# A long kernel transposed by the DMA crossbar, and 62 instead of 54 pairs of score tiles exponentiated on VectorE

## The chip, the cores and the metric

The kernel runs on one core of one Trainium2 chip. The core has five engines with their own instruction streams: TensorE (PE: matmuls and weight loads), VectorE (DVE), ScalarE (ACT), GpSimd (POOL) and SyncE (SP, which here only issues DMAs). The metric is the device time of one execution in microseconds. Before the change it is 924.57 us, the median of three runs (921.49 to 927.49).

## The reference, cut to what matters

The input `x` (2048 tokens, 640 features, bf16) goes through two branches, which a gate mixes token by token. Branch A multiplies a short causal convolution of `k` with `v`, and then convolves the product along the tokens with a kernel as long as the sequence, one for each feature (`ssm_k`, 640 x 2048). Branch B is attention with 32 heads of 20 features that share one key and one value.

```python
g = sigmoid((x * gate_w).sum(-1, keepdims=True))
# A: kv = shortconv(k) * v;  y = causal_conv(kv, ssm_k) (by FFT in the reference) + kv * ssm_D;  a = x * y
# B:
q = (x @ wq).reshape(B, S, 32, 20).transpose(0, 2, 1, 3)
k = x @ wk                                   # one key, one value for all heads
v = x @ wv
p = softmax(einsum("bhqd,bkd->bhqk", q, k) * 20 ** -0.5)
b = einsum("bhqk,bkd->bhqd", p, v).transpose(0, 2, 1, 3).reshape(B, S, 640) @ wo
return g * a + (1 - g) * b
```

## The kernel before

A Python program builds a graph of all operations with priorities and estimated costs, simulates the engines, and so fixes the order of the instructions on each engine before anything runs. On the chip each engine goes through its list in that order; an instruction whose input is late holds up all behind it.

The scores are made transposed, 128 keys by 512 queries of one head: a tile. A group is one block of 512 queries and four heads. There are 4 blocks and 8 sets of heads, so 32 groups, each with 16 key blocks `j` for each of its 4 heads: 2048 tiles in all. ScalarE takes most of them through `exp`, in units of three and two tiles by turns:

```python
n = 2 if len(self.units) % 2 else 3
...
op("act", lambda e: e.activation(et(n)[:, 0:w], self.ps[:, lo:lo + w], ACT.Exp, scale=SCALE), ...)   # L1056
```

TensorE writes the scores (`score`, L1024) into PSUM banks 0 to 2 and 3 to 4 and multiplies the exponentials with the values (`PVmm`, L1098) into bank 6, which collects one group. The banks 5 and 7 are for everything else.

Some key blocks of a group have two of their four heads on VectorE. `DVE_J[G]` lists these blocks. A pair is computed with integer and floating-point steps that build `exp` from an exponent and a polynomial, 128 x 1024 elements at a time:

```python
DVE_J = [()] * 5 + [(2, 9)] * 27
...
def DEXP(G, j):
    ...
        self.evac(gr, "dve", ...tensor_scalar(J[:, 512*h:512*h+512], self.bank(bk), ...))      # L1086, twice
    V(tensor_scalar(E, J, 7, 0x7F800000, logical_shift_left, bitwise_and), ...)                # L1089
    V(scalar_tensor_tensor(Ef, lo, ED, Ef, ALU.add, ALU.mult), ...)                            # L1091
    V(scalar_tensor_tensor(Jf, lo, EP, lo, ALU.add, ALU.mult), ...)                            # L1093
    V(scalar_tensor_tensor(T["ETd"], Jf, EQ, Ef, ALU.add, ALU.mult), ...)                      # L1094
```

There are two buffers `dJ`, one `dE` and one `ETd`. The value products of a pair may come at any point after the group's first one and must come before its last one (`late_pv`). When a group is full, VectorE copies bank 6 to `acc` (L1152), the denominators go through three small DMAs (`den`, `scr_d`, `rbc`), and VectorE scales the result (L1164).

The long convolution is done by discrete Fourier transforms, that is matmuls with tables of cosines and sines, in five blocks `c` of 128 features. It needs `ssm_k` with the tokens on the partitions. Each block is loaded as it lies, transposed on TensorE and copied out of PSUM by VectorE:

```python
def ssm_kT(self, c, base):
    p = c % 2
    st, kt = T["kst0"], T[f"ssm_kT{p}"]
    self.dma(st[:, :], self.aps["A_ssm_k"][CW*c:CW*c+CW, :], writes=[("kst", 0)], nbytes=524288, prio=base - 100, ...)
    for blk in range(2):
        gr = self.group("sk", base - 20 + blk)
        for n in range(NF):                                    # 8 transposes of 128 x 128, L1290
            self.mm(gr, lambda e, bk, ...: e.transpose(self.bank_bf(bk, 128, 128*n), st[:, j0:j0+128], T["ident"]), ...)
        self.evac(gr, "dve", ... e.tensor_copy(out, self.bank_bf(bk, 1024)), (), [("ssm_kT", p)], 0.7)   # L1293
```

The spectra (L1344, evicted by L1355, L1361 and L1363 on VectorE), their products (L1375, on GpSimd) and the inverse (L1408) follow, as side work between the exponentials. Two other inputs come in through transposing DMAs (`dma_start_transpose`) already: `xT` (L723) and `kTr` (L1254). Where TensorE has no side work, fillers (L1490: matmuls with zeros) stand in.

Of the kernel before, what the change touches and what calls it, by code (L numbers as in the profile page):

```python
# [10 lines left out]
BF16 = dt.bfloat16  # L11
# [486 lines left out]
S, D, H, DH = 2048, 640, 32, 20  # L498
NSC, NDC, NB = 16, 5, 4
L = 2048  # L500
NF = 8
CW = 128
# [7 lines left out]
UP = 256.0  # L510

SIDE = (7, 5)
DVE_J = [()] * 5 + [(2, 9)] * 27
MAC_ALT = ()
SCALE = float(DH) ** -0.5

# [25 lines left out]
class Kernel:  # L542

    def __init__(self, nc, aps):
        self.nc = nc
        self.aps = aps
        self.g = Graph()
        self.T = {}
        self.late_pv = []
# [52 lines left out]
    def alloc(self):  # L602
        nc = self.nc
        T = self.T

        def sb(name, shape, dtype):
            T[name] = nc.alloc_sbuf_tensor(name, shape, dtype)

        def size(shape, dtype):
            n = mybir.dt.size(dtype)  # L610
            for s in shape[1:]:
                n *= s
            return (n + 31) // 32 * 32

        def region(name, *sets):
# [3 lines left out]
            for st in sets:  # L619
                off = base  # L620
                for n, s, d in st:
                    T[n] = nc.alloc_sbuf_tensor_at(n, s, d, offset=off)
                    off += size(s, d)
# [55 lines left out]
        spec = []  # L679
# [2 lines left out]
        spec += [("Pp", [128, 3, 2, 2, CW], F32)]  # L682
        for i in range(2):
            spec += [(f"ssm_kT{i}", [128, 2, NF, CW], BF16)]
        spec += [("kst0", [128, S], BF16)]
        last = [("wo", [128, NDC, D], BF16), ("oTp0", [128, NDC, 512], BF16), ("oTp1", [128, NDC, 512], BF16)]
        last += [(f"outsb{i}", [128, D], BF16) for i in range(4)]
        region("R2", keep + early0, keep + early, spec + late, last)
        def over(name, under, off, shape, dtype):
            T[name] = nc.alloc_sbuf_tensor_at(name, shape, dtype, offset=nc.lookup_mloc(T[under]).addr + off)  # L690

# [2 lines left out]
        over("wog", "wq_pad", 0, [128, 8, D], BF16)  # L694
        self.fam0 = [n for n, _, _ in early0]
        self.early_fams = [n for n, _, _ in early + keep]
        self.late_fams = ["AB", "X", "K", "Pp", "ssm_kT", "kst"]
        self.spec_fams = ["X", "K", "Pp", "ssm_kT", "kst"]
        self.last_fams = ["wo", "oTp", "outsb"]
        self.ps = nc.alloc_psum_tensor("ps", [128, 4096], F32)  # L700
        self.ps_bf = self.ps[:, :].bitcast(BF16)
# [4 lines left out]
    def loads(self):  # L706
        T, aps = self.T, self.aps
        x = aps["A_q"][0].rearrange("(i p) d -> p i d", p=128)
        self.dma(T["wkv"][:, :, 0:20], aps["B_wk"].rearrange("(dc p) c -> p dc c", p=128), writes=["wk"],
                 nbytes=50000, eng="act", prio=-98.8)  # L710
        self.dma(T["wkv"][:, :, 20:40], aps["B_wv"].rearrange("(dc p) c -> p dc c", p=128), writes=["wv"],
                 nbytes=50000, eng="act", prio=-98.7)
        wq = aps["B_wq"].rearrange("(dc p) n -> p dc n", p=128)
        self.dma(T["gw5"][:, :], aps["gate_w"].rearrange("(dc p) -> dc p", p=128), writes=["gw5"], nbytes=2000,
                 eng="act", prio=-98.65)
        self.dma(T["wqst"][:, :, 0:160], wq[:, :, 0:160], writes=[("wqst", 0)], nbytes=204800, eng="act", prio=-98.6)
        xl = None
        x = aps["A_q"][0].rearrange("(i p) d -> p i d", p=128)
        self.dma(T["xn"][:, 12:16, :], x[:, 12:16, :], writes=[("xn", 3)], nbytes=655360, prio=-9)
        for b in range(NB - 1):  # L720
            o = T["xT"][:, :, 512 * b:512 * b + 512]
            i = aps["A_q"][0][512 * b:512 * b + 512, :]
            xl = self.g.add("sp", lambda e, o=o, i=i: e.dma_start_transpose(o, i), (), [("xT", b)], 0.1, kind="d",  # L723
                            nbytes=655360, prio=-8 + b, lat=1.6)
            xl.iss = 3.3

        self.xl = [xl]
        self.dma(T["wqst"][:, :, 160:640], wq[:, :, 160:640], writes=[("wqst", 1)], nbytes=614400, prio=-4,
                 after=self.xl)
        self.dma(T["Dbc"][:, :], aps["A_ssm_D"].partition_broadcast(128), writes=["Dbc"], nbytes=163840, prio=30,  # L730
                 after=self.xl)
# [262 lines left out]
    def stream(self):  # L994
# [4 lines left out]
        for G in range(8 * NB):  # L999
            for j in range(NSC):  # L1000
                mine = order
                if j in DVE_J[G]:
                    mine, rest = order[:2], order[2:]
# [11 lines left out]
    def attention(self):  # L1015
# [87 lines left out]
        def PV(G, j, rs):  # L1103
# [13 lines left out]
            if j == 0:  # L1117
                for jd in DVE_J[G]:
                    DEXP(G, jd)
# [158 lines left out]

    def ssm_kT(self, c, base):

        T = self.T
        p = c % 2
        st, kt = T["kst0"], T[f"ssm_kT{p}"]
        self.dma(st[:, :], self.aps["A_ssm_k"][CW * c:CW * c + CW, :], writes=[("kst", 0)], nbytes=524288,
                 prio=base - 100, name="ld_ssmk")
        for blk in range(2):
            gr = self.group("sk", base - 20 + blk)
            for n in range(NF):
                j0 = 128 * (NF * blk + n)
                self.mm(gr, lambda e, bk, n=n, j0=j0: e.transpose(self.bank_bf(bk, 128, 128 * n), st[:, j0:j0 + 128],  # L1290
                                                                  T["ident"][:, :]), [("kst", 0), "ident"], 0.09)
            out = kt[:, 1 - blk, :, :].rearrange("p n c -> p (n c)")
            self.evac(gr, "dve", lambda e, bk, out=out: e.tensor_copy(out, self.bank_bf(bk, 1024)), (),  # L1293
                      [("ssm_kT", p)], 0.7)

    def conv(self):
        T = self.T
# [251 lines left out]
```

## Time and profile before

| | before |
|---|---|
| measured, median of 3 (lowest to highest) | 924.57 us (921.49 to 927.49) |
| profiled span | 916.6 us |
| busy: TensorE, VectorE, ScalarE, GpSimd | 862.6, 572.5, 894.3, 369.0 us |
| wide and narrow exponentials on ScalarE | 388 and 388 |
| pairs on VectorE | 54 |
| transposes of the long kernel on TensorE | 80, 7.9 us busy |
| their copies on VectorE | 10, 6.9 us busy |

How to read the profile: a row of groups names the line of the program, the engine, the operation, the written and read tiles with their shapes, the count, the busy time and the mean duration; behind the second bar stands the time that the engine sat idle just before these instructions and what ended it. A row of waits reads "who waited <- for whom: total us, times, longest". A row of the timeline has start, duration, engine, line and operation, and in square brackets the idle time just before. A row of the windows has the stretch, then the busy time and number of instructions of PE, PEld (weight loads), DVE, ACT and POOL, then the granted clock, the DMA share and GB/s. The profiled span leaves out part of what the measured time holds, so the two are not compared with one another.

### The profile page before, as it was taken

Reading aid. Unit: us, or ns where it says so; the run is one execution under the profiler, and the core shown is the slowest. Engines: PE = TensorE matmul, PEld = TensorE weight load, DVE = VectorE, ACT = ScalarE, POOL = GpSimd, SP = SyncE. Lnnn points to the kernel's source line nnn. Section 1 sums busy time; section 2 is a strip of 40 time slices with the busy share of each in tenths; the row PEclk is TensorE's granted clock in tenths of the full one; section 3 lists DMA queues with packets and bytes.
Section 4 is the critical chain, followed back from the end, with each engine's and each line's share of the span. In section 5 each row is a group of like instructions: output and inputs, shape, how many; then the busy total and the mean of one; then the engine's idle time right before and its main releaser. Section 6 shows DMA issues by size and latency. Waiting matters only on the chain.

```text
span 916.6 us, 16425 instructions
## 1 busy us (share of the span) xinstructions
PE 862.6 (94%) x7024; PEld 355.5 (39%) x7086; DVE 572.5 (62%) x816; ACT 894.3 (98%) x800; POOL 369.0 (40%) x330
## 2 busy tenths in 40 slices
PE   7999999999999999999999999999999999988997
PEld 3344444443433434443343343433444333422332
DVE  6457743577666766567866777566676664466642
ACT  5999999999999999999999999999999999999995
POOL 2930055683234386234386234677243673000000
PEclk9999999999999999999999999999999999999999
DMA  7930100010000010000010010000000003002111
GB/s 161 205 128 6 56 28 20 14 31 18 18 19 20 14 35 15 19 20 19 15 38 10 28 46 19 14 18 9 18 20 19 13 14 85 23 28 63 34 34 37
DMA packets 48667, 32.69 MB, mean 36 GB/s; under 512 B 30674, under 2 KB 43986, under 8 KB 48594
## 3 DMA queue, kind: packets, MB, share of 16 engines
q1 hardware_dynamic: 46328, 31.05, 12.0%
q8 instruction: 55, 0.90, 0.4%
q10 hardware_dynamic: 2266, 0.59, 0.3%
q14 instruction: 18, 0.15, 0.1%
HBM read 20.64 MB, written 6.02 MB: 29 GB/s over the span
## 4 chain that ended last, share of the span: by engine, by line
ACT 59%; PE 34%; SPq 2%; DVE 2%; DMA 2%; issue 0%; DVEq 0%
ACT ETA L1056 36%; ACT ETB L1056 23%; PE ps L1024 10%; PE ps L1344 8%; PE ps L1098 7%; PE ps L1408 4%; PE ps L950 2%; SPq L1254 1%; PE ps L1271 1%; DVE ETd L1094 1%; DMA kTr<-in_A_k_dram 1%; PE ps L1188 1%; PE ps L1442 1%; DMA xT<-in_A_q_dram 1%; PE ps L966 1%; SPq L723 1%
## 5 line engine op out<-in xcount | busy, mean ns | idle before, releaser
L1056 ACT ACTIVATE ETA<-ps 128x1536 bf16<-128x1536 f32 x388 | 579.7, 1494 | 3.4 <-PE ps L1024 1.8
L1056 ACT ACTIVATE ETB<-ps 128x1024 bf16<-128x1024 f32 x388 | 417.7, 1077 | 0.0
L1024 PE MATMUL ps<-qT,kT 21*128 21x512 bf16 x2048 | 308.7, 384 | 33.2 <-ACT ETA L1056 16.3
L1375 POOL TENSOR_TENSOR Pp<-X,K 128x512 f32<-128x512 bf16 x120 | 163.3, 1386 | 355.9 <-DVE K L1363 354.7
L1098 PE MATMUL ps<-ETB,vaug 128*32 128x512 bf16 x776 | 200.2, 389 | 0.0
L1098 PE MATMUL ps<-ETA,vaug 128*32 128x512 bf16 x1164 | 191.7, 390 | 0.3 <-ACT ETB L1056 0.2
L1024 PEld LDWEIGHTS ps<-qT,kT 21*128 21x128 bf16 x2048 | 76.0, 91 | 215.4 <-ACT ETA L1056 114.8
L1094 DVE SCALAR_TENSOR_TENSOR ETd<-dJ,dE 128x1024 bf16<-128x1024 f32 x54 | 77.7, 1439 | 27.7 <-PE ps L1098 27.5
L1086 DVE TENSOR_SCALAR dJ<-ps 128x512 uint32<-128x512 f32 x108 | 74.1, 686 | 32.7 <-PE ps L1024 32.1
L1375 POOL TENSOR_TENSOR AB<-Pp 128x256 bf16<-128x256 f32 x80 | 78.0, 975 | 5.8
L1408 PE MATMUL ps<-AB,Tcos 128*128 128x256 bf16 x320 | 78.6, 275 | 0.2 <-issue 0.2
L1098 PEld LDWEIGHTS ps<-ETA,vaug 128*32 128x32 bf16 x1164 | 47.6, 92 | 66.6 <-issue 64.8
L1091 DVE SCALAR_TENSOR_TENSOR dE<-dJ,dE 128x1024 f32<-128x1024 uint16 x54 | 72.9, 1350 | 0.1
L1408 PE MATMUL ps<-AB,Tsin 128*128 128x256 bf16 x280 | 70.0, 275 | 0.0
L1093 DVE SCALAR_TENSOR_TENSOR dJ<-dJ 128x1024 f32<-128x1024 uint16 x54 | 68.4, 1267 | 0.1
L1098 PEld LDWEIGHTS ps<-ETB,vaug 128*32 128x32 bf16 x776 | 48.3, 93 | 47.1 <-issue 46.9
L1375 POOL TENSOR_TENSOR Pp<-Pp 128x512 f32<-128x512 f32 x40 | 57.4, 1434 | 3.1
L1152 DVE COPY acc<-ps 128x512 f32<-128x512 f32 x31 | 21.4, 691 | 58.9 <-PE ps L1098 58.9
L1344 PE MATMUL ps<-ssm_kT,Tcos 128*128 128x256 bf16 x320 | 53.0, 275 | 0.1
L1344 PE MATMUL ps<-kv,Tsin 128*128 128x256 bf16 x320 | 52.7, 275 | 0.0
L1344 PE MATMUL ps<-ssm_kT,Tsin 128*128 128x256 bf16 x320 | 52.7, 275 | 0.0
L1344 PE MATMUL ps<-kv,Tcos 128*128 128x256 bf16 x320 | 52.1, 275 | 0.4 <-DVE dJ L1086 0.4
(138 smaller groups left out, 842.4 us busy)
## 6 DMA issues: line engine op xcount, KB each, us to landing
rbc<-scr_d SPq DMA_DIRECT2D x31, 256.0 KB
scr_o<-oTn SPq DMA_DIRECT2D x24, 128.0 KB, 1.7
xn<-in_A_q_dram SPq DMA_DIRECT2D x4, 640.0 KB
kv<-in_A_v_dram SPq DMA_DIRECT2D x4, 640.0 KB
kst<-in_A_ssm_k_dram SPq DMA_DIRECT2D x5, 512.0 KB
out_dram<-outsb SPq DMA_DIRECT2D x14, 160.0 KB, 1.8
oTp<-scr_o SPq DMA_DIRECT2D x12, 160.0 KB, 3.3
wog<-in_B_wo_dram SPq DMA_DIRECT2D x4, 200.0 KB
```

The costliest lines, as they stand in the source:

```text
L950: o = self.mm(gr, lambda e, bk, gi=gi, dc=dc: e.matmul(self.bank(bk), T["wq_pad"][:, dc, 128 * gi:128 * gi + 128], T["xT"][:, dc, 512 * I: ...
L1024: return e.matmul(self.bank(bk), T["kT4"][32 * r:32 * r + 21, 128 * j:128 * j + 128], T[f"qT{G // 8 % 2}"][32 * r:32 * r + 21, G % 8, :], ...
L1056: op("act", lambda e: e.activation(et(n)[:, 0:w], self.ps[:, lo:lo + w], ACT.Exp, scale=SCALE), [("ps", base[n % 2] + k) for k in range(le ...
L1086: self.evac(gr, "dve", lambda e, bk, h=h: e.tensor_scalar(J[:, 512 * h:512 * h + 512], self.bank(bk), SCALE * LOG2E * 65536.0, EOFF * 6553 ...
L1091: V(lambda e: e.scalar_tensor_tensor(Ef, lo, ED, Ef, ALU.add, ALU.mult), [kJ, "dE"], ["dE"], c_ps(1024), **k)
L1093: V(lambda e: e.scalar_tensor_tensor(Jf, lo, EP, lo, ALU.add, ALU.mult), [kJ], [kJ], c_ps(1024), **k)
L1094: V(lambda e: e.scalar_tensor_tensor(T["ETd"][:, :], Jf, EQ, Ef, ALU.add, ALU.mult), [kJ, "dE"], ["ETd"], c_ps(1024), **k)
L1098: return op("pe", lambda e: e.matmul(self.bank(6)[32 * r:32 * r + 32, :], T["vaug"][:, j, :], src, start=(j == 0), stop=(j == NSC - 1), ti ...
L1152: self.dve(lambda e: e.tensor_copy(T["acc"][:, :], self.bank(6)), [("ps", 6)], ["acc"], c_ps(512), prio=-9000.0, name="acc")
L1344: o = self.mm(gr, lambda e, bk, lhs=lhs, rhs=rhs, comp=comp, n=n: e.matmul(self.bank(bk, 256, 256 * comp), lhs, rhs, start=(n == 0), stop= ...
L1375: f = lambda e: e.tensor_tensor(out, a, b, alu)
L1408: self.mm(gr, lambda e, bk, lhs=lhs, fc=fc, comp=comp, h=h: e.matmul(self.bank(bk, 256, 256 * h), lhs, AB[:, fc, :, comp, :], start=(fc == ...
```

## The change

Two things change. First, the long kernel is loaded by transposing DMAs straight from DRAM into `ssm_kT`, two of 128 features by 1024 tokens for each block; the staging tile `kst0`, the transposes on TensorE and the copies on VectorE go. Second, `DVE_J` gives VectorE 62 pairs instead of 54, and no longer the same two key blocks in each group: groups 3 and 5 get one pair, group 6 four, groups 7, 12, 23, 27, 28, 30 and 31 three, group 22 one, and the other groups from 8 on two. It is meant to relieve ScalarE, and to make room for that on VectorE and TensorE.

```diff
-DVE_J = [()] * 5 + [(2, 9)] * 27
+DVE_J = [(), (), (), (6,), (), (2,), (3, 7, 11, 13), (2, 6, 11), (2, 9), (2, 9), (2, 9), (2, 9), (3, 8, 13), (2, 9), (2, 9), (2, 9), (2, 9), (2, 9), (4, 11), (2, 9), (3, 9), (2, 9), (2,), (3, 8, 13), (2, 9), (2, 7), (2, 9), (2, 7, 12), (3, 8, 13), (3, 9), (3, 8, 13), (2, 7, 12)]
@@ alloc
-        spec += [("kst0", [128, S], BF16)]
@@ ssm_kT
-        st, kt = T["kst0"], T[f"ssm_kT{p}"]
-        self.dma(st[:, :], self.aps["A_ssm_k"][CW * c:CW * c + CW, :], writes=[("kst", 0)], nbytes=524288, ...)
         for blk in range(2):
-            gr = self.group("sk", base - 20 + blk)
-            for n in range(NF):
-                j0 = 128 * (NF * blk + n)
-                self.mm(gr, lambda e, bk, n=n, j0=j0: e.transpose(...), [("kst", 0), "ident"], 0.09)
-            out = kt[:, 1 - blk, :, :].rearrange("p n c -> p (n c)")
-            self.evac(gr, "dve", lambda e, bk, out=out: e.tensor_copy(out, self.bank_bf(bk, 1024)), ...)
+            o = self.T[f"ssm_kT{p}"][:, 1 - blk, :, :]
+            i = self.aps["A_ssm_k"][CW * c:CW * c + CW, 1024 * blk:1024 * blk + 1024]
+            x = self.g.add("sp", lambda e, o=o, i=i: e.dma_start_transpose(o, i), (), [("ssm_kT", p)], 0.1, kind="d",
+                           nbytes=262144, prio=base - 100, lat=1.9, name="ld_ssmk")
+            x.iss = 1.5
```

(The lists of tile families lose `kst` too.)

More of the change, by code (lines that the diff above doesn't have):

```diff
@@ L696, in alloc @@
         self.early_fams = [n for n, _, _ in early + keep]
-        self.late_fams = ["AB", "X", "K", "Pp", "ssm_kT", "kst"]
-        self.spec_fams = ["X", "K", "Pp", "ssm_kT", "kst"]
+        self.late_fams = ["AB", "X", "K", "Pp", "ssm_kT"]
+        self.spec_fams = ["X", "K", "Pp", "ssm_kT"]
         self.last_fams = ["wo", "oTp", "outsb"]
@@ L1279, in ssm_kT @@
     def ssm_kT(self, c, base):
-        T = self.T
         p = c % 2
-        st, kt = T["kst0"], T[f"ssm_kT{p}"]
-        self.dma(st[:, :], self.aps["A_ssm_k"][CW * c:CW * c + CW, :], writes=[("kst", 0)], nbytes=524288,
-                 prio=base - 100, name="ld_ssmk")
         for blk in range(2):
-            gr = self.group("sk", base - 20 + blk)
-            for n in range(NF):
-                j0 = 128 * (NF * blk + n)
-                self.mm(gr, lambda e, bk, n=n, j0=j0: e.transpose(self.bank_bf(bk, 128, 128 * n), st[:, j0:j0 + 128],
-                                                                  T["ident"][:, :]), [("kst", 0), "ident"], 0.09)
-            out = kt[:, 1 - blk, :, :].rearrange("p n c -> p (n c)")
-            self.evac(gr, "dve", lambda e, bk, out=out: e.tensor_copy(out, self.bank_bf(bk, 1024)), (),
-                      [("ssm_kT", p)], 0.7)
+            o = self.T[f"ssm_kT{p}"][:, 1 - blk, :, :]
[3 more added lines that the diff above has]
+            x.iss = 1.5
     def conv(self):
```

## The prediction

> **What bounds the kernel now.** I read the page first (shares, slices, the largest groups), then ScalarE's waits, then the starts of all 776 exponentials in order of time, then VectorE's rows and one stretch where ScalarE did stall. The page:
>
> ```profile
> span 916.6 us, 16425 instructions
> PE 862.6 (94%) x7024; PEld 355.5 (39%) x7086; DVE 572.5 (62%) x816; ACT 894.3 (98%) x800; POOL 369.0 (40%) x330
> ...
> ACT  5999999999999999999999999999999999999995
> ...
> L1056 ACT ACTIVATE ETA<-ps 128x1536 bf16<-128x1536 f32 x388 | 579.7, 1494 | 3.4 <-PE ps L1024 1.8
> L1056 ACT ACTIVATE ETB<-ps 128x1024 bf16<-128x1024 f32 x388 | 417.7, 1077 | 0.0
> L1094 DVE SCALAR_TENSOR_TENSOR ETd<-dJ,dE 128x1024 bf16<-128x1024 f32 x54 | 77.7, 1439 | 27.7 <-PE ps L1098 27.5
> L1086 DVE TENSOR_SCALAR dJ<-ps 128x512 uint32<-128x512 f32 x108 | 74.1, 686 | 32.7 <-PE ps L1024 32.1
> L1091 DVE SCALAR_TENSOR_TENSOR dE<-dJ,dE 128x1024 f32<-128x1024 uint16 x54 | 72.9, 1350 | 0.1
> L1093 DVE SCALAR_TENSOR_TENSOR dJ<-dJ 128x1024 f32<-128x1024 uint16 x54 | 68.4, 1267 | 0.1
> L1089 DVE TENSOR_SCALAR dE<-dJ 128x1024 uint32<-128x1024 uint32 x54 | 48.1, 891 | 0.2
> ```
>
> ScalarE is full in 38 of 40 slices, and its exponentials waited 3.4 us in all. The reader should see that TensorE's 94% is not a second bound of the same kind: 105 of its matmuls (L1490, 35.0 us) are fillers on zeros that keep its clock up, and ScalarE's own list of waits names it hardly at all:
>
> ```profile
> ACT ETA L1056 <- PE ps L1024: 1.8, 4, 0.8
> ...
> ACT ETA L1056 <- PE ps L1098: 0.7, 1, 0.7
> ```
>
> In the timeline of ScalarE the exponentials stand 1.345 us (1536 columns) and 0.915 us (1024 columns) apart from start to start, 2.26 us for five tiles of 512. So the span is a sum: first exponential at 24.0, then 388 x 2.26 = 876.9, plus 6.4 us by which the starts stand further apart than that, ending at 907.5, plus a tail of 9.1 (last value product, transposes, projection, store): 916.4 of 916.6. Of the 6.4 us, 0.85 falls at 41 us (startup), 0.52, 0.39 and 0.64 at 449, 476 and 722 us, and the rest is a gap of 0.1 to 0.2 about every sixth pair of exponentials, whatever else is going on.
>
> The three middle gaps are the ones that concern this change. This is the first:
>
> ```profile
> 446.35 1.33 POOL L1375 TENSOR_TENSOR Pp<-Pp 128x512 f32<-128x512 f32 x1
> ...
> 446.53 2.24 DVE L1094 SCALAR_TENSOR_TENSOR ETd<-dJ,dE 128x1024 bf16<-128x1024 f32 x1
> ...
> 448.82 0.10 PEld L1098 LDWEIGHTS ps<-ETd,vaug 128*32 128x32 bf16 x2 [0.92 <-DVE ETd L1094]
> ...
> 450.29 1.45 ACT L1056 ACTIVATE ETA<-ps 128x1536 bf16<-128x1536 f32 x1 [0.35 <-PE ps L1024]
> ```
>
> VectorE's last step of a pair took 2.24 us where its median is 1.225, because GpSimd was at work; TensorE, whose order is fixed, waited 0.92 us at the value product of that pair; ScalarE ran out of scores for 0.35 us.
>
> **What the Trainium skill says.** "ScalarE: Activation LUTs", section "What ACT_TABLE_LOAD costs", gives an ACTIVATE 0.833 ns an element and a lane beside a fixed part. The trace agrees: (1.345 - 0.915) us over 512 columns is 0.84 ns a column, and the fixed part left is 0.055 us. "SBUF — State Buffer", section "Who interferes with whom", says that VectorE and GpSimd share a port pair, that a VectorE instruction with two SBUF inputs contends with a GpSimd instruction that reads SBUF, and that whoever comes second waits out the whole instruction. The trace agrees: the ETd step has 1160/1225/2340 ns as shortest, median and longest, and the slow one above begins under a GpSimd instruction. "DMA: Bandwidth & Descriptors", section "DMA Transpose (X-bar)", has the transpose issued from SP or ScalarE only, two-byte, into SBUF, and warns of two streams that transpose at once. All transposes here stay on SP, one stream. The trace has seven of them already:
>
> ```profile
> L1254 SPq DMA_TRANSPOSE kTr<-in_A_k_dram x4: 3363/4652/4995, 23.7 to 38.6; - x4
> ...
> DMA to landing us min/median/max: 5.4/5.4/5.4
> ```
>
> **The change part by part.** *Fewer tiles on ScalarE.* There are 32 groups x 16 key blocks x 4 heads = 2048 tiles. Before, 54 pairs, 108 tiles, go to VectorE: 1940 = 388 x 5. After, 62 pairs: 2048 - 124 = 1924 = 384 x 5 + 3 + 1. Four double units go (4 x 2.26 = 9.04), and a unit of three (1.345) and one of one (0.915 - 0.43 = 0.485, an estimate from the slope) stay of them: 9.04 - 1.83 = 7.2 us off the chain that sets the end. This is the whole direct gain.
>
> *More on VectorE.* One pair costs 2 x 686 + 891 + 1350 + 1267 + 1439 = 6.32 us as a mean. Eight more: 50.6 us. The removed copies of the long kernel (ten at 687 ns) give 6.9 back. VectorE goes from 572.5 to about 616 us of about 909, 68%. As a sum it fits. Where it is dense is the question: the first eight groups go from six pairs to nine, with four in group 6 and three in group 7, and groups 12, 23, 27, 28, 30 and 31 have three. A group with 2, 3, 4 pairs lasts (64 - 4, 6, 8 tiles) x 0.452 = 27.1, 26.2, 25.3 us.
>
> *Transposes on TensorE go.* 80 matmuls, 7.9 us by their row, and ten PSUM slots in the two side banks. They lie between exponentials in side work that ScalarE did not wait for; 7.2 us less time for side work is about balanced by 7.9 us less of it. Gain on the path: none that I can point to.
>
> *Transposes by DMA.* Ten of 256 KB in place of five loads of 512 KB. From the 3.4 to 5.0 us of issue and 5.4 us to landing of 640 KB, 40% of the bytes should take an estimated 1.4 to 2 us of SP's queue and under 5 us to land. The two parities of the target are free long before they are read: the load before was issued at 99.9 us and its first use as a spectrum began at 117.6 us. Off the path.
>
> **The rivals.** *First, VectorE late at the value products.* The windows of time show group 6 before, with two pairs:
>
> ```profile
> 190.40:217.60 27.20, 26.64 (x218) 11.20 (x217) 21.88 (x25) 27.20 (x25) 22.96 (x17) 1.00 0.05 16
> ```
>
> VectorE is busy 21.88 of 27.2 us there (third number), GpSimd 22.96 (fifth). Two more pairs would make 34.5 in 25.3 us. What speaks against a collapse: a pair can be computed before its group begins, as the queries lie ready, and only the last step waits for the ETd buffer. So of four pairs only the last step of the second and all of two more, about 14 us, must lie inside; spectra and other side evictions can slip. And groups 4 and 5 before it hold one pair between them. What speaks for it: already with two pairs three groups stalled ScalarE. If each of the eight dense groups stalls twice by 0.5 us, 8 us go and the time is 925, no change. If VectorE simply can't keep up and groups wait for several us each, 945.
>
> *Second, TensorE as the true bound.* In the convolution its windows are full to 26.2 to 27.1 of 27.2 us, and the chain of waits gives it 34%. If side work already pushes scores back, the 7.2 us shrink. Against it: 2.5 us of waits on TensorE in 884 us, and late windows with 1 to 4 us of fillers each. It would make 921 to 923.
>
> *Third, the crossbar is slow or holds up SP.* The chain of the denominators (three small DMAs a group) shares SP. A delay of some us there has most of a 27 us group to vanish in. Even 20 us to landing would be hidden. It would show only if the spectra of a block started late: under 1 us.
>
> *Fourth, more than the direct gain.* At most the three middle gaps (1.5 us) vanish as well: 915.9.
>
> **Range and chances.** Less 7.2 us direct. I add 1.5 us for new stalls: the five dense groups inside the convolution (6, 7, 12, 23, 27), where GpSimd contends, cost an estimated 0.5 us each, the mean of the three gaps seen, and I take 1 us of it back for the placing, which was evidently picked group by group and can have taken the old gaps away. Three groups at the end have no GpSimd work. So -5.7 us: the profiled span goes to about 910.9, the measured median of 924.57 to 918.8. The measurements of before lie 6 us apart, so the range is 913.5 to 924.5. Two per cent is 18.5 us: faster by that would need 11 us more than ScalarE's work loses, slower by that 25 us of new stalls; hence 0.02, 0.93 and 0.05.
>
> **What would show it.** Right, if the profile after has 385 wide exponentials and 385 narrow ones (one of 512 columns), VectorE near 616 us, and ScalarE's starts 2.26 us apart nearly throughout with the sum of gaps at 6 to 9 us. The first rival shows as ScalarE waiting on scores with TensorE waiting on ETd just ahead, in groups 6 and 7 (196 to 248 us) above all. The second shows as ScalarE waiting for TensorE with no ETd ahead. The third shows as waits for ssm_kT by a DMA. I am wrong if waits of ScalarE grow by over 5 us, or if anything outside the exponentials (24.0 us before, 9.1 us behind) moves by more than 1 us.

## The result, and the profile after

The changed kernel takes 911.63 us, the median of four executions (910.80 to 912.68), against 924.52 us of the kernel before in the same comparison (four executions, 921.49 to 927.49): ratio 0.986, 95% interval 0.983 to 0.990. The prediction had 918.8 us and a range of 913.5 to 924.5. The time fell by 12.9 us, and the prediction had 5.7. (The ratios in this document leave out executions over 1.5% above the fastest one of their kernel, so they understate what the longest executions cost; medians and ranges have them all.)

The page of the changed kernel, whose lines lie one or eight further up in the program (L1055 for L1056, L1336 for L1344):

```profile
span 910.4 us, 16325 instructions
...
PE 853.5 (94%) x6958; PEld 352.7 (39%) x7015; DVE 608.0 (67%) x854; ACT 887.8 (98%) x794; POOL 370.2 (41%) x330
...
ACT  5999999999999999999999999999999999999995
...
L1055 ACT ACTIVATE ETA<-ps 128x1536 bf16<-128x1536 f32 x385 | 570.4, 1481 | 2.1 <-PE ps L1023 1.0
L1055 ACT ACTIVATE ETB<-ps 128x1024 bf16<-128x1024 f32 x385 | 408.7, 1062 | 0.1
```

The profiled span is 910.4 us, and the prediction had put it at 910.9. ScalarE has 385 units of each kind, as counted, and waits 2.2 us for scores instead of 3.4. Its sum, read from the starts as before: first exponential at 25.6 us (24.0 before), last one ends at 901.2 (907.5), tail 9.2 (9.1). Between first and last, 875.6 us against 883.5: 7.2 from the eight pairs, and gaps of 5.8 us in place of 6.4.

So the profiled spans differ by 6.2 us, and the measured medians by 12.9. The two are of different executions. The profiled execution of the kernel before took 918.4 us as measured, 1.8 more than its span, and the profiled one of the changed kernel 912.2, again 1.8 more. The four timed executions of the kernel before were 3 to 9 us longer than its profiled one. What the four timed ones had in them is the question of the experiments.

### The profile page after: what moved, and what is told of

Its sections match the earlier page's. It is cut to its first block, busy times and chain, and to the rows that moved or that the text cites. A ratio compares the mean times of both kernels' runs of the same rounds, so it can differ in the third digit from the quotient of the medians.

```text
span 910.4 us, 16325 instructions
## 1 busy us (share of the span) xinstructions
PE 853.5 (94%) x6958; PEld 352.7 (39%) x7015; DVE 608.0 (67%) x854; ACT 887.8 (98%) x794; POOL 370.2 (41%) x330
## 3 DMA queue, kind: packets, MB, share of 16 engines
q1 hardware_dynamic: 56168, 31.05, 12.6%
## 4 chain that ended last, share of the span: by engine, by line
ACT 73%; PE 24%; DVE 1%; DMA 1%; SPq 1%; issue 0%; DVEq 0%
ACT ETA L1055 44%; ACT ETB L1055 29%; PE ps L1023 7%; PE ps L1336 5%; PE ps L1097 5%; PE ps L1400 3%; PE ps L949 2%; DVE ETd L1093 1%; DMA xT<-in_A_q_dram 1%; SPq L722 1%; PE ps L965 0%; PE ps L893 0%; PE ps L1270 0%; PE ps L1482 0%; PE ps L1211 0%
## 5 line engine op out<-in xcount | busy, mean ns | idle before, releaser
L1055 ACT ACTIVATE ETA<-ps 128x1536 bf16<-128x1536 f32 x385 | 570.4, 1481 | 2.1 <-PE ps L1023 1.0
L1055 ACT ACTIVATE ETB<-ps 128x1024 bf16<-128x1024 f32 x385 | 408.7, 1062 | 0.1
L1023 PE MATMUL ps<-qT,kT 21*128 21x512 bf16 x2048 | 303.5, 384 | 37.5 <-ACT ETA L1055 22.4
L1097 PE MATMUL ps<-ETA,vaug 128*32 128x512 bf16 x1155 | 195.6, 389 | 0.3 <-ACT ETB L1055 0.3
L1097 PE MATMUL ps<-ETB,vaug 128*32 128x512 bf16 x769 | 186.8, 389 | 0.0
L1085 DVE TENSOR_SCALAR dJ<-ps 128x512 uint32<-128x512 f32 x124 | 85.2, 687 | 39.1 <-PE ps L1023 38.6
L1093 DVE SCALAR_TENSOR_TENSOR ETd<-dJ,dE 128x1024 bf16<-128x1024 f32 x62 | 85.9, 1385 | 24.1 <-PE ps L1097 23.8
L1090 DVE SCALAR_TENSOR_TENSOR dE<-dJ,dE 128x1024 f32<-128x1024 uint16 x62 | 83.1, 1340 | 0.3
L1092 DVE SCALAR_TENSOR_TENSOR dJ<-dJ 128x1024 f32<-128x1024 uint16 x62 | 81.5, 1314 | 0.2
L1088 DVE TENSOR_SCALAR dE<-dJ 128x1024 uint32<-128x1024 uint32 x62 | 53.6, 865 | 0.6
L1336 PE MATMUL ps<-ssm_kT,Tsin 128*128 128x256 bf16 x320 | 53.0, 275 | 0.0
L1336 PE MATMUL ps<-kv,Tcos 128*128 128x256 bf16 x320 | 51.7, 275 | 0.2 <-issue 0.2
L1336 PE MATMUL ps<-ssm_kT,Tcos 128*128 128x256 bf16 x320 | 51.8, 275 | 0.0
```

The costliest lines, as they stand in the source:

```text
L1023: return e.matmul(self.bank(bk), T["kT4"][32 * r:32 * r + 21, 128 * j:128 * j + 128], T[f"qT{G // 8 % 2}"][32 * r:32 * r + 21, G % 8, :], ...
L1085: self.evac(gr, "dve", lambda e, bk, h=h: e.tensor_scalar(J[:, 512 * h:512 * h + 512], self.bank(bk), SCALE * LOG2E * 65536.0, EOFF * 6553 ...
L1088: V(lambda e: e.tensor_scalar(E[:, :], J[:, :], 7, 0x7F800000, ALU.logical_shift_left, ALU.bitwise_and), [kJ], ["dE"], c_fast(1024), **k)
L1090: V(lambda e: e.scalar_tensor_tensor(Ef, lo, ED, Ef, ALU.add, ALU.mult), [kJ, "dE"], ["dE"], c_ps(1024), **k)
L1092: V(lambda e: e.scalar_tensor_tensor(Jf, lo, EP, lo, ALU.add, ALU.mult), [kJ], [kJ], c_ps(1024), **k)
L1093: V(lambda e: e.scalar_tensor_tensor(T["ETd"][:, :], Jf, EQ, Ef, ALU.add, ALU.mult), [kJ, "dE"], ["ETd"], c_ps(1024), **k)
```

## The experiments

**The two parts alone, and both kernels again.** Four kernels on one chip. Theory A says that VectorE's lateness, as in the prediction's first rival, comes and goes from execution to execution; B, that TensorE's granted clock does; C, that the span leaves out a fixed part which is larger for the kernel before.

```diff
 # d1_dma_only: the change without its new pairs
-DVE_J = [(), (), (), (6,), ...]
+DVE_J = [()] * 5 + [(2, 9)] * 27
 # p1_pairs_only: the kernel before with the new pairs
-DVE_J = [()] * 5 + [(2, 9)] * 27
+DVE_J = [(), (), (), (6,), ...]
```

The kernel before:

> The kernel before, unchanged, to see how far its executions differ. Theory A (hidden stalls: its measured executions contain some 6 us of ScalarE stalls that the one profiled execution of 916.6 us happened not to have): the spans spread from about 916 to 926 us at a granted clock of 1.00, and a profile of a longer one shows more or longer gaps between the exponentials than 6.4 us. Theory B (clock: TensorE was throttled in the measured executions): the spans go with the granted clock, below 0.99 where they are long. Theory C (a fixed offset between span and measured time that is larger for this kernel): spans near 916.6 in every run, measured 924.

The crossbar transposes alone:

> Only the DMA transposes; the 54 pairs at their old places. By the prediction they are worth nothing on the path: ratio to before 1.000, within 0.003. If the transposes on TensorE, with their two PSUM slots and their copies on VectorE, caused the hidden stalls of theory A, 918 to 920 us and a small spread (ratio 0.993 to 0.995).

The pairs alone:

> Only the 62 pairs at the new places; the long kernel still transposed on TensorE. By the prediction's sum: 7.2 us less, 917 us, ratio 0.992. If the old places of the pairs caused the hidden stalls: 912 us, as the whole change, ratio 0.986. If new stalls eat some of it without the relief of the transposes: 919 to 923.

The changed kernel again:

> The changed kernel, unchanged, on the same chip as the three others: 911 to 913 us, ratio 0.986, spans of 909 to 911 us, a spread under 3 us. If it also spreads to 917 and more here, the difference of the first measurement was partly chance.

| kernel | executions | lowest, median, highest (us) | ratio to before (95%) |
|---|---|---|---|
| before | 12 | 916.6, 918.6, 934.9 | 1.000 (0.998 to 1.002) |
| transposes alone | 11 | 917.0, 923.6, 925.6 | 1.006 (1.004 to 1.008) |
| pairs alone | 4 | 911.1, 912.7, 930.3 | 0.994 (0.993 to 0.996) |
| the change | 9 | 912.4, 916.8, 924.8 | 0.999 (0.996 to 1.002) |

Here the change brings nothing that can be measured, and the transposes alone cost. Theory C falls at once: one and the same program has executions 6 to 12 us apart. The nine of the changed kernel lie at about 912, 917 and 921 to 925; nine of the eleven with the transposes alone lie at 923 to 926 and two at 917. These are steps, not a spread, and the mean granted clock of each execution, which is on record, goes with them: 0.998 in the three of the changed kernel at 912 us, 0.988 in the three at 917, 0.977 to 0.983 in the three at 921 to 925. With the transposes alone it is 1.000 in the two at 917 us and 0.987 to 0.990 in the nine others.

A profile fell on a long execution of the changed kernel (span 923.0 us). Two rows of its slices, ScalarE's busy tenths and the granted clock:

```profile
ACT  5999799999999999999999999999999988999996
...
PEclk9998799999999999999999999999999977999999
```

The clock is down in two places, and ScalarE is less than full just there. In stretches of 5 us the second place looks so (the third number from the end is the clock, 1.00 is full):

```profile
741.00:746.00 5.00, 5.00 (x45) 2.16 (x43) 0.69 (x1) 5.00 (x6) 4.99 (x5) 1.00 0.01 3
746.00:751.00 5.00, 3.68 (x34) 1.23 (x31) 1.60 (x3) 5.00 (x5) 5.00 (x6) 1.00 0.01 1
751.00:756.00 5.00, 5.00 (x23) 1.04 (x20) 4.67 (x4) 4.36 (x5) 5.00 (x4) 0.51 0.02 2
756.00:761.00 5.00, 5.00 (x23) 0.80 (x21) 2.97 (x3) 3.28 (x4) 4.73 (x4) 0.50 0.14 52
...
771.00:776.00 5.00, 5.00 (x42) 2.38 (x40) 1.82 (x2) 4.77 (x5) 0.00 (x0) 0.94 0.46 130
```

From 746 to 751 us TensorE is busy for 3.68 of 5 us. Then the clock goes to one half and stays there until about 772 us, although TensorE is now busy without a break; it gets 23 instructions done in 5 us where it did 45, and ScalarE runs 3.28 us of 5. Its waits in this execution, in full the two longest:

```profile
ACT ETA L1055 <- PE ps L1023: 7.1, 9, 1.4
ACT ETA L1055 <- PE ps L1097: 6.1, 6, 1.8
```

That is 13.2 us of waiting where the shorter execution had 1.2, and the gaps between the starts add up to 20.4 us instead of 5.8. The span is 12.6 us longer (14.6 of gaps, less 2.0 by which the first exponential came earlier). VectorE's busy time is the same to a tenth (608.0). This is theory B. The Trainium skill, "TensorE: Matmul & The Clock Gate", section "What's actually happening", says that an activity monitor grants half or full clock by how busy TensorE has been in a window that runs freely, not tied to the kernel's start. The trace agrees as to one half: no kept profile has another value than 1.00 and 0.50. It also shows a fixed beat. In each profile with several falls and rises behind the first exponential, all of them lie on one grid of 3.41 us (17 stretches in the one without fillers, further below), and against the first instruction the grid lies elsewhere in another execution. Such a grid would fit an effect that comes and goes: a thin place of a few us falls into one window in one execution, and is cut in two in the next. The page puts the release after about 3.4 us of sustained work; here the half clock lasts some 21 us of it, and the measurement decides.

The same 5 us in the profile of 910.4 us hold TensorE's thinnest place too, a few us earlier, and the clock stays up:

```profile
736.00:741.00 5.00, 5.00 (x43) 2.20 (x44) 0.69 (x1) 5.00 (x5) 4.98 (x5) 1.00 0.01 3
741.00:746.00 5.00, 3.42 (x30) 1.15 (x29) 2.61 (x4) 5.00 (x5) 5.00 (x6) 1.00 0.02 2
746.00:751.00 5.00, 4.41 (x32) 1.20 (x31) 4.97 (x5) 4.97 (x6) 4.92 (x4) 1.00 0.06 10
```

So a thin place is a risk, not a cost in each execution.

The first place of the long execution, at 86 us, is another matter:

```profile
80.50:85.50 5.00, 4.28 (x46) 1.95 (x47) 4.04 (x8) 5.00 (x5) 0.00 (x0) 1.00 0.02 2
85.50:106.00 20.50, 20.50 (x150) 10.98 (x148) 7.17 (x12) 14.03 (x13) 0.00 (x0) 0.50 0.07 21
```

TensorE was busy for 4.28 of the 5 us before, and other places of the same profile with less (3.94 of 5 us from 833.5 us on) kept the full clock. So busy time by the profile orders the risk only roughly. This stretch also began before the first crossbar transpose of that execution was issued (105.9 us).

**Is the weak activity the cause?** A second set on another chip: the transposes alone again, more fillers, no fillers.

```diff
 # d3_dma_fill80 (transposes alone) and a2_fill80 (the change): a filler goes in where TensorE
 # was busy for less than this share of the 2.4 us before
-FILL = 0.55
+FILL = 0.80
 # a3_nofill (the change)
-        sch.filler = lambda e: e.matmul(self.bank(6), self.T["zeros"][:, :], ...)
+        sch.filler = None
```

> The DMA transposes alone once more, unchanged, to catch a profile of an execution of 923 us: nine of its eleven executions took 923 to 926 us and the profiled one 917. Theory B (the clock): executions lie in steps of 6 to 7 us, and a profile of 923 us shows one stretch of about 20 us at half the granted clock, with ScalarE waiting for TensorE there; the gaps outside it stay at 5 us. Theory A (late VectorE): the clock is 1.00 throughout and ScalarE's gaps lie behind late ETd steps.

> The DMA transposes alone, with about twice as many filler matmuls (319 instead of 163 in the program). Theory B, with weak activity of TensorE as the trigger: the executions of 923 us go, all at 916 to 918 us. Theory A: no change of the spread, or longer, as TensorE has more to do.

> The whole change with about twice as many fillers (308 instead of 151). Theory B: all executions at 910 to 913 us, none at 917 or 922 to 925 as without them. Theory A: the same spread as without, or some us more.

> The whole change without any filler matmuls behind the first exponential. Theory B: more stretches at half clock, several in each execution, each 6 to 7 us: 925 to 950 us, mean granted clock below 0.97. Theory A: 911 us or a little less, as TensorE has less to do and VectorE's lateness is the same.

| kernel | executions | lowest, median, highest (us) | ratio to before (95%) |
|---|---|---|---|
| transposes alone | 20 | 916.6, 922.2, 925.4 | 1.002 (1.000 to 1.005) |
| transposes alone, more fillers | 20 | 919.6, 922.8, 926.5 | 1.004 (1.003 to 1.006) |
| the change, more fillers | 12 | 913.1, 917.3, 923.0 | 0.999 (0.996 to 1.002) |
| the change, no fillers | 4 | 969.6, 1012.1, 1033.1 | |

Without fillers the time goes up by 100 us, and the slices of the clock show where it went:

```profile
PEclk9799999999999988969799778969768599555556
```

Less work on TensorE, and a longer kernel: the fillers are not idle decoration, and theory A, which had expected 911 us or less, falls. The profile of the transposes alone (span 920.4 us) shows the step of 6 us that most of its executions have, in the same place as above:

```profile
741.00:746.00 5.00, 3.65 (x30) 0.96 (x28) 0.69 (x1) 5.00 (x5) 4.84 (x5) 1.00 0.02 2
746.00:751.00 5.00, 5.00 (x23) 0.91 (x21) 3.58 (x4) 3.96 (x5) 1.88 (x2) 0.51 0.31 82
751.00:756.00 5.00, 5.00 (x27) 1.26 (x25) 1.82 (x2) 3.68 (x3) 0.00 (x0) 0.50 0.77 158
```

One stretch of half clock of 14 us, behind 3.65 us of work in 5. But doubling the fillers did not help: theory B had expected the long executions to go, and the medians of 922.8 and 917.3 us are no better than without (922.2 here, 916.8 in the first set). The two profiles have the stretch as well, from 749 us on. The list of TensorE tells why. It puts no filler between the last value product of a group and the first of the next one, whatever `FILL` is, since the filler writes into the bank that VectorE is then reading. Near the end of the convolution such a boundary meets a stretch without side work: in the program's own schedule the changed kernel has 1.1 us of matmuls in its thinnest 3 us there, the transposes alone as well, and the kernel before and the pairs alone have 1.5 us at their thinnest. The traces agree. The place looks so in the kernel before (b1_before), in the change (the profile of 910.4 us) and with the transposes alone (d1_dma_only), in executions where the clock stayed up:

```profile
745.20:748.20 3.00, 2.28 (x22) 0.62 (x22) 1.99 (x2) 3.00 (x3) 3.00 (x4) 1.00 0.03 3
741.00:744.00 3.00, 1.68 (x17) 0.56 (x15) 1.60 (x3) 3.00 (x4) 3.00 (x5) 1.00 0.00 0
742.80:745.80 3.00, 1.65 (x15) 0.39 (x11) 0.69 (x1) 3.00 (x4) 2.88 (x3) 1.00 0.00 0
```

TensorE is busy for 2.28 of 3 us in the first, and for 1.68 and 1.65 in the others.

That is theory D: a thin place in TensorE's list, made by taking the transposes out. The transposes did not lie at that place themselves (in the kernel before they start between 108.7 and 610.7 us); without them the program puts the later side work in another order.

**A hole in the kernel before, and the hole closed in the change.** A third set, on a third chip:

```diff
 # h1_before_hole: the kernel before, three fillers fewer at one place of the list
-            if (self.filler is not None and ... and self.can_fill and m is not None and gap > 0.1
+            if (self.filler is not None and ... and self.can_fill and not 743 < t < 746 and m is not None and gap > 0.1
 # a4_side (the change) and d4_side (transposes alone): fillers between two groups too, in a free side bank
+            if (self.filler is not None and self.main_started and not self.can_fill and m is not None and gap > 0.1
+                    and self.busy_in(t, 2.4) < 0.85):
+                for x in SIDE:
+                    if not self.bank_claimed[x] and not self.bank_busy[x] and self.bank_ready[x] <= t:
+                        f = Op("pe", lambda e, x=x: self.fill_side(e, x), c_mm(512), "c", "fill", 0.0)
+                        f.deps.update(self.fill_deps)
+                        f.deps.update(self.bank_last[x])
+                        return f
```

> The kernel before with three fillers left out where the changed kernel's list of TensorE has its thinnest 3 us (at about 745 to 755 us of the trace), so that its thinnest place is as thin as there; nothing else of the change. Theory D (a thin place in TensorE's list near the end of the convolution, made by taking the transposes out, lets the clock fall to half for 14 to 21 us in a part of the executions): a good part of the executions take 922 to 925 us instead of 917, and a half-clock stretch in a profile lies at about 750 us. Rival E (the crossbar transposes themselves, or denser VectorE work, bring the clock down): 917 us as before, as it has neither.

> The whole change, with fillers also where the list had none: between the last value product of a group and the first of the next, in a free side bank (174 fillers instead of 169 in the list; the thinnest 3 us have 1.5 us of matmuls instead of 1.1). Theory D: the executions of 916 to 925 us become rare, median 911 to 913 us, ratio to before 0.993 to 0.995. Rival E: the same spread as the change alone, median 915 to 918.

> The DMA transposes alone, with the same extra fillers. Theory D: most executions at 917 us instead of 922 to 924, ratio 1.000. Rival E: median 922 to 923, as without.

> The changed kernel, unchanged, on the chip of the three others, as their control: under theory D a mixture of 911 to 913 us and of executions 5 to 7 us and 10 to 13 us longer; profile either with no half-clock stretch and about 910 us, or with one at about 750 us and 916 us or more.

| kernel | executions | lowest, median, highest (us) | ratio to before (95%) |
|---|---|---|---|
| before with the hole | 6 | 926.2, 928.7, 938.3 | 1.011 (1.006 to 1.015) |
| the change, fillers between groups | 8 | 910.9, 913.7, 914.9 | 0.992 (0.989 to 0.995) |
| transposes alone, fillers between groups | 22 | 917.9, 922.3, 938.7 | 1.003 (1.001 to 1.005) |
| the change | 22 | 910.5, 920.8, 934.8 | 1.000 (0.997 to 1.002) |

Three matmuls with zeros taken out of some 16,000 instructions cost the kernel before 9 us, with nothing else of the change in it. The order of the instructions in the two traces (b1_before and this run) shows that the edit is as small as it sounds: VectorE, ScalarE and GpSimd have the same lists, and on TensorE four fillers at 749 to 751 us are gone, one stands 1.6 us later, and three weight loads of side work, with their matmuls, come a little later, behind the fall of the clock. All six executions have a clock of 0.970 to 0.984, where the median execution of the kernel before on that chip has 0.998. The loss is more than theory D had expected (922 to 925). The profile:

```profile
751.00:756.00 5.00, 3.68 (x25) 0.93 (x22) 5.00 (x7) 5.00 (x6) 1.80 (x2) 0.79 0.15 50
756.00:761.00 5.00, 5.00 (x22) 0.92 (x20) 3.63 (x4) 3.18 (x3) 3.45 (x3) 0.50 0.02 8
```

Once down, the clock stayed at one half there until 805 us. Rival E (the crossbar itself, or denser VectorE work) is not needed for this: the kernel has neither. The traces also speak against the crossbar in the other kernels: its last transpose of the long kernel was issued at 461 us with the transposes alone and at 489 us in the change, over 250 us before the stretches at 746 and 751 us.

With the boundary filled the changed kernel has all of its executions within 4 us, while the change without it, on the same chip, spreads over 24. This pair is less pure than the hole. The rule adds only five fillers on balance, but it moves much of the list: at least 232 of the 854 instructions of VectorE change their place in the order, and GpSimd's work ends at 740 us instead of 754. So it shows that a list without that thin place is steady, not that the five fillers alone make it so. The other half of the pair did not come out clean: the transposes alone still have 10 of 22 executions over 924 us, so here theory D missed. Their profile has a new thinnest place (1.77 us of work in the 3 us from 759 us on). That a thin place can bring the clock down is shown by the hole; a rule for how thin is too thin is not.

**The long executions of the kernel before.** A fourth set, with the same filler rule on the kernel before and on the pairs alone, and the best kernel again:

> The kernel before with the extra fillers in the free side banks (187 instead of 160 in the list; the thinnest 3 us 1.59 instead of 1.54 us). If the executions of 921 us and more of the kernel before (a quarter to a third of them, and all timed ones of the first comparison) are half-clock stretches that begin at thin places, their share falls and the median is 917 to 918. If they are something else (a disturbance from outside the core), their share stays at a quarter to a third.

> The 62 pairs alone, unchanged, with more executions than the four before. Its list of TensorE has no thin place below 1.52 us. Theory D: 911 to 914 us, ratio 0.993 to 0.995, few long executions. If the relief by the crossbar transposes were needed for the denser pairs, 914 us and more with a gap in ScalarE behind late ETd steps.

> The 62 pairs alone with the extra fillers: 911 to 914 us, ratio 0.992 to 0.995, the same as the whole change with the extra fillers if the crossbar transposes are worth nothing in themselves; 2 to 4 us more than it if they are worth their 8 us of TensorE time.

> The whole change with the extra fillers once more, on another set of executions: 911 to 915 us, ratio 0.991 to 0.995.

| kernel | executions | lowest, median, highest (us) | ratio to before (95%) |
|---|---|---|---|
| before | 58 | 917.2, 919.8, 955.9 | |
| before, fillers between groups | 22 | 915.6, 917.1, 920.7 | 0.996 (0.994 to 0.998) |
| pairs alone | 19 | 909.8, 915.3, 925.4 | 0.993 (0.990 to 0.996) |
| pairs alone, fillers between groups | 21 | 912.0, 915.6, 929.2 | 0.995 (0.992 to 0.997) |
| the change, fillers between groups | 9 | 911.9, 913.0, 915.8 | 0.992 (0.988 to 0.995) |

Of the 58 executions of the kernel before, 25 took over 921 us; with the fillers between groups none of 22 did. Over all four chips there are 190 executions of the kernel before with their clock on record. The 129 under 921 us have 0.996 to 1.000, the 56 of 923 us and more 0.947 to 0.993. So its long executions are half-clock executions too, and a list with more fillers, in another order, did not have them. The pairs alone are not free of it either, as theory D had expected them to be; their longest execution has two stretches at other places than 750 us, of 20.5 us from 86 us on (where the changed kernel had one, and with no crossbar transpose of the long kernel here) and of 17.1 us from 632 us on:

```profile
PEclk9998699999999999999999999996999999999999
```

And p3_pairs_side stayed as spread as p2_pairs_only. The change with fillers between groups, by contrast, is steady on both chips, 17 executions within 910.9 to 915.8 us, and beats both kernels: 0.992 of before, where the change itself is at 0.999 and 1.000 in the sets of its own later executions. Its profile, between the same microseconds (GpSimd's work, the fifth engine, is already over there):

```profile
736.00:741.00 5.00, 4.47 (x34) 1.49 (x33) 0.01 (x1) 5.00 (x5) 1.45 (x2) 1.00 0.42 107
741.00:746.00 5.00, 5.00 (x46) 2.42 (x44) 1.84 (x3) 5.00 (x6) 0.00 (x0) 1.00 0.28 73
746.00:751.00 5.00, 4.72 (x42) 1.88 (x41) 4.65 (x8) 5.00 (x6) 0.00 (x0) 1.00 0.70 180
```

## Why the prediction was right or wrong

**Where it failed.** The step is the last one of the sum: "the profiled span goes to about 910.9, the measured median of 924.57 to 918.8". It took the 8.0 us between the span of 916.6 and the median of 924.57 for something that any execution of any version carries. Only 1.8 of it is. With 1.8, the same working gives 912.7, and the four executions lie at 910.8 to 912.7. The other 6 us were in the timed executions of the kernel before, and most executions of that kernel, on four further occasions, do not have them: the lowest of each occasion is 916.6 to 917.2 us, and 129 of 190 are under 921. What the runs showed in its place is a clock that falls to half, mostly behind thin places of TensorE's list, and in the kept profiles with fillers for 14 to 21 us as a rule and once for 51; a stretch of 14 to 21 us costs some 4 to 7 us, and the one of 51 us in the kernel with the hole cost about 18 (the gaps between the exponentials add up to 24.4 us there).

The clock of those four executions is not on record, so that they had such stretches is inferred from the later ones, not seen. Luck alone does not explain the first comparison well either: of 31 later executions of the changed kernel 5 are as short as all of its first four were, and of 190 of the kernel before 57 are as long as all of its first four. If executions were drawn independently at these shares, four in a row would have a chance under 0.1% and one of 0.8% (an estimate from these counts). Something of that occasion must have differed too, as the shares do between the later chips (5 of 27 executions over 921 us on one, 25 of 58 on another). What it was stays open.

**The direct gain: right.** 7.2 us off ScalarE was the estimate, and 7.9 us less between first and last exponential is what the profile has, gaps included. (The gaps that the prediction listed leave out three of 0.31 to 0.38 us at 252, 293 and 498 us; its sum of 6.4 has them.) The lowest execution of each kernel in all sets, 916.6 and 910.5 us, lie 6.1 us apart.

**VectorE: right in kind, 8 us too high.** 608.0 us against 616. A pair costs 2 x 687 + 865 + 1340 + 1314 + 1385 = 6.28 us, so the pairs give 2.6 us of the difference; the rest lies in other rows.

**First rival, late value products: fell.** The three old gaps behind late ETd steps (0.52, 0.39, 0.64 us) are gone and two small ones (0.30 and 0.35, at 229 and 827 us) are new. The stretch that the prediction showed as group 6 lies some 7 us early; counted by its exponentials the group is this, in the kernel before,

```profile
197.60:224.80 27.20, 26.18 (x212) 10.53 (x211) 21.75 (x26) 27.20 (x25) 15.76 (x12) 1.00 0.05 16
```

and, with four pairs instead of two, in the changed kernel:

```profile
199.00:224.30 25.30, 24.30 (x195) 9.34 (x192) 22.93 (x29) 25.25 (x24) 5.66 (x5) 1.00 0.05 17
```

VectorE is busy 22.93 of 25.3 us, and ScalarE still 25.25. It was not asked for 34 us. Only three of the four last steps of a pair, and five of the eight first ones, fall into this stretch, so its rows of pair work add up to 17.2 us (13.7 before), and its other rows to 7.7 (9.4 before). GpSimd, which lives on the spectra that VectorE evicts, has 5.66 us there where it had 15.76. Pairs spread over the neighbouring groups and side work slips, as the prediction set against the rival.

**Second rival, TensorE as the bound: wrong form.** I weighed whether TensorE has too much work, saw fillers in the list and took them for slack. They were the sign that it can have too little. (The row of 105 that the prediction read is also incomplete: 142 weight loads of that line stand in the same trace, so matmul records are missing.) With that, "Gain on the path: none that I can point to" for the removed transposes missed that removing them could cost: the transposes alone are at 1.006, 1.002 and, with fillers between groups, 1.003.

**Third rival, the crossbar: off the path, as said.**

```profile
L1284 SPq DMA_TRANSPOSE ssm_kT<-in_A_ssm_k_dram x10: 1232/1274/1822, 99.7 to 482.2; - x10
...
DMA to landing us min/median/max: 3.5/3.5/3.6
```

1.27 us of SP's queue and 3.5 us to landing; the estimates were 1.4 to 2 and under 5. No engine waited for one of these DMAs.

**Startup.** "I am wrong if ... anything outside the exponentials moves by more than 1 us": the first exponential came 1.6 us later in that profile. The clock explains it. In the profile of 910.4 us it was at one half from 12.6 to 16.0 us; in another execution of the same kernel (a5_after) it was not, and the first exponential came at 23.8 us:

```profile
12.60:16.00 3.40, 3.10 (x26) 1.65 (x28) 2.13 (x10) 0.51 (x2) 0.00 (x0) 0.50 0.68 151
12.60:16.00 3.40, 3.34 (x28) 1.63 (x25) 2.62 (x11) 2.21 (x5) 0.00 (x0) 1.00 0.64 136
```

Four kept profiles have this stretch at the start, and their first exponentials come at 25.2 to 25.8 us. So it is a difference of executions, and not of the change.

## What to carry to other kernels

Before a difference of one per cent is given a cause, compare the measured time of the profiled execution with the timed ones: if they differ, the profile doesn't show what the median holds. Where the clock of TensorE depends on how busy it is, taking work off TensorE is a change of its own: look for the thinnest few us of its list and fill them, also where the usual filler is not allowed. Read the granted clock of each execution before comparing times. And a gain that lies in the list (here eight pairs at 0.9 us) shows in the lowest executions of several occasions, while half of a difference between two medians of four can come from the occasion.

## What the runs showed of the hardware

- The granted clock was 1.00 or 0.50 in all kept profiles, never between. In the four long executions with complete matmul records and with fillers (a1_after, d2_dma_again, d3_dma_fill80, a2_fill80) it fell after 5 us in which TensorE was busy 3.65 to 4.28 us by the profile, without an idle piece of 1 us. In another execution of a kernel with the same thin place (d1_dma_only, 3.46 of 5 us) it stayed at 1.00.
- Each stretch lasted a whole multiple of 3.41 us, with TensorE busy nearly throughout: 13.7 (transposes alone), 20.5 (the change) and 51.2 us (before with the hole).
- One stretch of 14 to 21 us costs this kernel, which ScalarE bounds, some 4 to 7 us, since ScalarE waits for scores meanwhile: 917 instead of 912 us in the first set with one stretch's worth of lost clock, and 13.2 us of waits in an execution with two.
- Three filler matmuls of 512 columns were worth 9 us; all of them together about 100 us.
